# Result products of the first 32 columns over all 128 feature rows, even columns before odd ones, in a dynamic convolution with a maxout block

## The chip, the cores and the metric

The kernel runs on one core of a Trainium2 chip. The metric is the time of one execution on the device in microseconds (us), the median of several runs.

## The reference

Two steps. The first is a dynamic convolution: every position of a sequence has its own 7 weights for each of 8 heads, a softmax of `weight_gen`. The second is a block with two linear maps whose larger value goes on.

```python
# x: (8, 4160, 192), weight_gen: (8, 4160, 8, 7), w1, w2: (192, 1024), w_out: (1024, 192)
w = softmax(weight_gen, axis=-1)                        # with 1e-9 in the denominator
x_pad = zeros(6 rows) followed by x, along the sequence
y[b, s, head] = sum over k in 0..6 of w[b, s, head, k] * x_pad[b, s + k, head]   # 24 features a head
h1 = y @ w1 ; h2 = y @ w2                               # 33280 rows
out = np.maximum(h1, h2) @ w_out                        # float32, (33280, 192)
```

## The kernel before

The 33280 rows lie on the 128 partitions, 260 rows to each. A *column* is one such row on all partitions, so it is 128 rows of the output; there are 260 columns (`NT`). They are worked on in batches of 16 (`BATCHES`), cut into units of 4 columns in the first two batches and of 8 afterwards (`UNITS`).

VectorE (DVE in the profile) multiplies the shifted x by the weights into `m_t` (`mul`, L182) and adds the seven taps into `y_t` (`adds`, L198 to L205). ScalarE (ACT) computes the softmax (L135, L151, L167) and the relus. A DMA transposes `y_t` into `yt` (L214); for the units of 4 columns TensorE (PE) transposes and sums at once instead (`sum_transpose`, L246), and ACT copies the result to `yt` (L253).

The maximum is written as max(h1, h2) = h1 + relu(h2 - h1). So TensorE forms the hidden values `y @ (w2 - w1)` (`hid_tile`, L297), ACT applies the relu (L307, into `rd_t`, with the feature row on the partition), and the result of a column is the sum of two parts in one bank of PSUM: `yt` times the small product w1 @ w_out (`w10`, L349, three products), and `rd_t` times `w_out` (`wo`, L337, in 8 chunks of 128 feature rows).

All products of the main part use half of the array's height: 64 of the 128 rows on which the sum runs. Two of them, one on rows 0 to 63 and one on rows 64 to 127, run side by side, into two different banks. For the results, columns c and c+1 form a pair: `out_first` sums the lower half of the rows into the bank of column c and the upper half into that of column c+1, and `out_second` does the other half of each. Between the two passes a bank goes from one half of the array to the other. `relay` puts an empty ScalarE instruction there, which waits for the last two products of the first pass, and the first two products of the second pass wait for it.

The order of work is written out by hand (a manual schedule). `GROUPS` are two or three hidden tiles each; `hidden` runs one group: all tiles but the last, `out_first` for the columns in turn (`OUTS[g]`, two or four of them), their relus, the relay, the last tile, softmax steps, its relu, `out_second`, and `evac`, the copy of the results from PSUM to `o_t` by ACT (L393), stored by a DMA. The columns 0 to 31 are finished between about 27 and 79 us. At the opening, before 27 us, TensorE runs some products that use the full height: `keep_warm` (L610), `w1_transposed` (L598, its first eight) and `w10_product` (L652).

Of the kernel before, what the change touches and what calls it, by code (L numbers as in the profile page):

```python
# [23 lines left out]
def kernel(  # L24
# [11 lines left out]
    B, S, D = x.shape  # L36
    H, K = weight_gen.shape[2], weight_gen.shape[3]
    F = moe_w1.shape[1]
    P = 128
    PAD = K - 1  # L40
    WGC = H * K
    FCH = F // P
# [190 lines left out]
    def half(j):  # L233
        return slice(64 * j, 64 * j + 64)
# [75 lines left out]
    def column(c):  # L310

        b = min(c // 16, NB - 1)
        for u, (ub, o, n) in enumerate(UNITS):
            if ub == b and o <= c - BATCHES[b][0] < o + n:
                k = c - BATCHES[b][0] - o
                return u, k // 2, k % 2
# [7 lines left out]
    def op_out(c):  # L324

        tile_, at = op_at[c // 2]
        return tile_[:, at + c % 2 * 512:at + c % 2 * 512 + D]

    def out_hidden(c, f, r):

        u, i, j = column(c)
        t0 = TILES.index((u, 0))
        if UNITS[u][2] == 8:
            (rd, k), at = rd_at[t0 + f], j * 512 + i * P
        else:
            (rd, k), at = rd_at[t0 + f // 2], j * 512 + f % 2 * 256 + i * P
        return nc.tensor.matmul(  # L337
            op_out(c), lhsT=rd[half(r), k * 1024 + at:k * 1024 + at + P],
            rhs=wo[half(r), f * D:(f + 1) * D], start=False, stop=(r != j and f == FCH - 1),
            skip_group_check=True,  # L340
        )

    def out_first(now):

        for c in now[::2]:
            u, i, _ = column(c)
            for s in range(3):
                for j in range(2):
                    nc.tensor.matmul(  # L349
                        op_out(c + j),  # L350
                        lhsT=yt_ts[u][half(j), (3 * i + (s + j) % 3) * P:(3 * i + (s + j) % 3 + 1) * P],
                        rhs=w10[half(j), s * D:(s + 1) * D], start=(c == now[0] and s == 0),
                        stop=False, skip_group_check=True,
                    )
            for f in range(FCH):
                last = [out_hidden(c + j, f, j) for j in range(2)]
        return last

    def out_second(now, go):

        for c in now[::2]:
            for f in range(FCH):
                for j in range(2):
                    mm = out_hidden(c + 1 - j, f, j)
                    if c == now[0] and f == 0:
                        tc.add_manual_dep(mm.ins, go.ins.name, SYNC, reason="bank of the other half")

    def relay(last):

        go = nc.scalar.nop()  # L370
        for mm in last:
            tc.add_manual_dep(go.ins, mm.ins.name, SYNC, reason="bank of the other half")
        return go
# [52 lines left out]
    OUTS, c = [[], [], []], 0  # L426
# [8 lines left out]
    def room(g):  # L435

        t0, n = GROUPS[g]
        if "c" in ps:
            for t, k in zip(range(t0, t0 + n), "abc"[:n - 1] + "c"):
                hd_at[t] = ps[k].tile([P, 1024], FP32, name="hd" + k, tag=k), 0  # L440
        else:
            for t in range(t0, t0 + n):
                hd_at[t] = ps["h"].tile([P, 1024], FP32, name="hdp", tag="hd"), 0
        rd = prd.tile([P, 3 * 1024], BF16, name="rd_t", tag="rd")
        for t in range(t0, t0 + n):
            rd_at[t] = (rd, t - t0)
        return rd
# [7 lines left out]
    def hidden(g, now=(), between=lambda: None, beside=lambda: None, ahead=lambda: None,  # L455
               before=lambda: None, after=lambda: None, begun=None):


        t0, n = GROUPS[g]
        rd = begun or room(g)  # L460
        for t in range(t0, t0 + n - 1) if not begun else ():
            hid_tile(t)
        if now:
            out_room(now, "a" if n == 1 and "a" in ps else None)
            last = out_first(now)
        for t in range(t0, t0 + n - 1) if not begun else ():
            relu(rd, t, 1)
        if now:
            go = relay(last)
        hid_tile(t0 + n - 1)  # L470
        before()
        if len(now) > 2:
            beside()
        relu(rd, t0 + n - 1, 1)
        ahead()
        if now:
            out_second(now, go)
            evac(now[0] // 2, len(now) // 2)
        between()
        after()  # L480
        if len(now) <= 2:
            beside()

    def rest_of_results(c):

        parts = [p for p in (c[:4], c[4:-2], c[-2:]) if p]
        assert max(map(len, parts)) <= 4
        go = []
        for i, now in enumerate(parts):
            out_room(now, ("r", "a", "c")[i])  # L490
            go.append(relay(out_first(now)))
            if i:
                out_second(parts[i - 1], go[i - 1])
                evac(parts[i - 1][0] // 2, len(parts[i - 1]) // 2)
        out_second(parts[-1], go[-1])
        evac(parts[-1][0] // 2, len(parts[-1]) // 2)
# [4 lines left out]
    wo = consts.tile([P, FCH * D], BF16, name="wo")  # L501
# [7 lines left out]
    with tc.tile_pool(name="pstage", bufs=1) as pstage:  # L509
# [120 lines left out]
        rd = room(0)  # L630
# [43 lines left out]
        rd = room(3)  # L674
# [11 lines left out]
        sum_transpose(3)  # L686
        out_room(OUTS[3])
        go = relay(out_first(OUTS[3]))
        exp_sum(2)
        red(2)  # L690
        weights(1, 8)
        rd = room(4)
# [113 lines left out]
```

## Time and profile before

| what | value |
|---|---|
| median of 3 runs | 406.31 us (406.18 to 407.36) |
| the profiled execution | 406.16 us, span of its profile 404.3 us |
| TensorE matmul, busy | 397.3 us (98%), 7458 instructions |
| VectorE, busy | 370.3 us (92%) |
| ScalarE, busy | 360.7 us (89%) |
| GpSimd, busy | 76.3 us (19%) |
| L337, the result products | 210.3 us busy, 4160 instructions |
| L297, the hidden products | hda 67.0, hdb 67.0, hdc 67.8 us busy, and hdp at the opening |
| L349, the first part of the results | 55.3 us busy, 780 instructions |

The profile is one execution, taken by the hardware profiler. In its lines PE is TensorE's matmul, PEld its weight load, DVE is VectorE, ACT ScalarE, POOL GpSimd and SP the engine that issues DMAs. A group line gives the source line, the engine, the operation, what is written and read, the shapes (64*128 is the height and width of the array that a matmul uses), how many there are, their busy time and the mean duration of one in ns, and the idle time of the engine before them. Since matmuls are pipelined, their durations overlap; what one costs is the distance from its start to the next start.

### The profile page before, as it was taken

What the parts mean: (1) busy time and instruction counts of PE and PEld (TensorE: products, weight loads), DVE (VectorE), ACT (ScalarE), POOL (GpSimd) and SP (SyncE); (2) the same over time, 40 slices, a digit from 0 to 9 for tenths busy, and PEclk for the clock granted to TensorE, in tenths of its full rate; (3) what the DMA queues carried; (4) which work ended last, traced back from release to release, by engine and by line L of the source; (5) the groups of instructions that cost most, each with busy time, mean ns of one, the idle gap of its engine ahead of it and who ended that gap; (6) DMA issues with size and microseconds to landing.
All of it is one profiled execution on the core that took longest, in us unless ns stands there. A gap on an engine that the chain in (4) does not pass through costs nothing.

```text
span 404.3 us, 16242 instructions
## 1 busy us (share of the span) xinstructions
PE 397.3 (98%) x7458; PEld 318.6 (79%) x7458; DVE 370.3 (92%) x215; ACT 360.7 (89%) x462; POOL 76.3 (19%) x101
## 2 busy tenths in 40 slices
PE   7999999999999999999999999999999999999996
PEld 2699999777777787778777778877787877777795
DVE  5999999999999999999999999999999999999100
ACT  6899999999999989999899999989999899897872
POOL 0311130212222011222221212222012222110000
PEclk9999999999999999999999999999999999999999
DMA  8956549876757855774775587577548647743614
GB/s 250 232 120 184 157 98 245 149 174 155 194 90 232 191 111 121 229 204 78 233 201 109 115 237 203 74 236 200 110 111 240 170 70 241 154 89 51 246 41 158
DMA packets 60785, 65.70 MB, mean 163 GB/s; under 512 B 47631, under 2 KB 49039, under 8 KB 60718
## 3 DMA queue, kind: packets, MB, share of 16 engines
q1 hardware_dynamic: 52334, 40.54, 35.6%
q0 software_dynamic: 8240, 24.04, 29.2%
q8 instruction: 58, 0.95, 0.9%
q10 hardware_dynamic: 144, 0.10, 0.1%
q14 instruction: 9, 0.07, 0.1%
HBM read 35.96 MB, written 25.56 MB: 152 GB/s over the span
## 4 chain that ended last, share of the span: by engine, by line
PE 92%; ACT 3%; DMA 2%; SPq 1%; issue 0%; DVE 0%; DVEq 0%; ACTq 0%
PE op_ps L337 42%; PE hdc L297 13%; PE hda L297 13%; PE hdb L297 13%; PE op_ps L349 8%; PE yps L246 2%; DMA ws1T<-in_moe_w_dram 2%; ACT rd_t L307 1%; PE hdp L297 1%; SPq L544 0%; ACT yt L253 0%; PE pw L652 0%; ACT w1t L670 0%; ACT e_t L135 0%; SPq L536 0%
## 5 line engine op out<-in xcount | busy, mean ns | idle before, releaser
L337 PE MATMUL op_ps<-wo,rd_t 64*128 64x192 bf16 x4160 | 210.3, 243 | 0.0
L337 PEld LDWEIGHTS <-rd_t 64*128 64x128 bf16 x4160 | 180.6, 94 | 15.5
L182 DVE TENSOR_TENSOR m_t<-xb_t,en_t 128x10752 bf16<-128x10752 bf16 (+1 forms) x37 | 187.4, 5070 | 0.3
L297 PEld LDWEIGHTS <-wd 64*128 64x128 bf16 x1776 | 93.4, 94 | 40.1 <-issue 1.1
L307 ACT ACTIVATE rd_t<-hdc 128x1024 bf16<-128x1024 f32 x82 | 84.0, 1024 | 17.6 <-PE hdc L297 15.9
L222 POOL CAST gate<-yt 128x1 f32<-128x1 bf16 x29 | 41.1, 1416 | 267.3 <-DMA yt<-y_t 267.3
L307 ACT ACTIVATE rd_t<-hdb 128x1024 bf16<-128x1024 f32 x81 | 83.6, 1032 | 0.0
L307 ACT ACTIVATE rd_t<-hda 128x1024 bf16<-128x1024 f32 x81 | 83.4, 1030 | 0.0
L198 DVE TENSOR_TENSOR m_t<-m_t 128x4608 bf16<-128x4608 bf16 (+1 forms) x29 | 72.7, 2508 | 0.1
L297 PE MATMUL hdc<-yt,wd 64*128 64x512 bf16 (+1 forms) x534 | 67.8, 359 | 0.0
L393 ACT COPY o_t<-op_ps 128x384 f32<-128x384 f32 (+1 forms) x99 | 56.3, 579 | 12.6 <-PE op_ps L337 12.6
L297 PE MATMUL hda<-yt,wd 64*128 64x512 bf16 (+1 forms) x528 | 67.0, 359 | 0.0
L297 PE MATMUL hdb<-yt,wd 64*128 64x512 bf16 (+1 forms) x522 | 67.0, 362 | 0.0
L349 PE MATMUL op_ps<-w,yt 64*128 64x192 bf16 x780 | 55.3, 243 | 0.0
L349 PEld LDWEIGHTS <-yt 64*128 64x128 bf16 x780 | 38.8, 94 | 15.6 <-issue 0.5
L202 DVE TENSOR_TENSOR m_t<-m_t 128x3072 bf16<-128x3072 bf16 (+1 forms) x29 | 49.9, 1722 | 0.1
L167 ACT ACTIVATE en_t<-wg_t 128x896 bf16<-128x896 f32 (+2 forms) x45 | 35.2, 809 | 2.0 <-PE op_ps L337 2.0
L205 DVE TENSOR_TENSOR y_t<-m_t 128x1536 bf16<-128x1536 bf16 (+1 forms) x29 | 27.3, 941 | 0.5
L114 POOL DMA_DIRECT2D xb_t<-in_x_dram x33 | 18.0, 546 | 21.3 <-DVE m_t L182 10.4
L156 DVE TENSOR_TENSOR wg_t<-wg_t,sum_t 128x280 f32<-128x280 f32 (+5 forms) x46 | 22.0, 481 | 0.0
L147 DVE TENSOR_REDUCE sum_t<-e_t 128x64 f32<-128x448 f32 (+2 forms) x31 | 19.5, 633 | 2.3 <-ACT e_t L135 2.3
L135 ACT ACTIVATE e_t<-wg_t 128x896 f32<-128x896 f32 (+2 forms) x18 | 15.9, 889 | 2.3 <-DMA wg_t<-in_weight_gen_dram 2.3
(49 smaller groups left out, 117.1 us busy)
## 6 DMA issues: line engine op xcount, KB each, us to landing
out_dram<-o_t SPq DMA_DIRECT2D x27, 768.0 KB, 4.5
xb_t<-in_x_dram POOLq DMA_DIRECT2D x30, 384.0 KB, 4.9
wg_t<-in_weight_gen_dram POOLq DMA_DIRECT2D x14, 448.0 KB, 5.6
xb_t<-xb_t POOLq DMA_DIRECT2D x16, 288.0 KB, 5.1
out_dram<-o_t SPq DMA_DIRECT2D x10, 384.0 KB, 3.1
wg_t<-in_weight_gen_dram SPq DMA_DIRECT2D x2, 448.0 KB, 4.2
xs<-in_x_dram SPq DMA_DIRECT2D x2, 384.0 KB, 6.0
xb_t<-in_x_dram POOLq DMA_DIRECT2D x3, 192.0 KB, 4.6
```

The source lines that it names most:

```text
L156: nc.vector.tensor_tensor(out=w_t, in0=w_t, in1=_sub(s_ts[b], hs.start, [[1, hs.stop - hs.start], [0, K]]), op=ALU.subtract)
L167: nc.scalar.activation(out=_sub(en_ts[b], (o * WGC + j * N * K) * 2, [[2 * N, K], [2, N], [1, 2]]), in_=_sub(wg_ts[b], (o * H + j * N) * K ...
L182: return nc.vector.tensor_tensor(out=m_out, in0=x_in, in1=_sub(en_ts[b], o * WGC * 2, [[2, K * n * H], [0, G // 2], [1, 2]]), op=ALU.mult,)
L198: nc.vector.tensor_tensor(out=taps(0, 1, 3), in0=taps(0, 1, 3), in1=taps(3, 1, 3), op=ALU.add)
L202: nc.vector.tensor_tensor(out=taps(0, 2, 2), in0=taps(0, 2, 2), in1=taps(1, 5, 2), op=ALU.add)
L205: nc.vector.tensor_tensor(out=_sub(y_ts[b], o * D, [[64, 2], [P, 3 * w // 2], [1, 64]]), in0=taps(0, 1, 1), in1=taps(2, 1, 1), op=ALU.add,)
L222: nc.gpsimd.tensor_copy(out=gate, in_=yt[:, 0:1])
L297: nc.tensor.matmul(hid_out(t, f, j), lhsT=wd_at(j, s, f // 4, f % 4 * P, P), rhs=_sub(yt_ts[u][half(j), :], (s + j) % 3 * P, [[3 * P, w // ...
L307: relu_of[t0] = nc.scalar.activation(out=rd[:, k * 1024:(k + n) * 1024], in_=hd[:, at:at + n * 1024], func=AF.Relu)
L337: return nc.tensor.matmul(op_out(c), lhsT=rd[half(r), k * 1024 + at:k * 1024 + at + P], rhs=wo[half(r), f * D:(f + 1) * D], start=False, s ...
L349: nc.tensor.matmul(op_out(c + j), lhsT=yt_ts[u][half(j), (3 * i + (s + j) % 3) * P:(3 * i + (s + j) % 3 + 1) * P], rhs=w10[half(j), s * D: ...
L393: nc.scalar.copy(out=_sub(o, c % 24 * D, [[D, len(qs)], [h * D, 2], [1, D]]), in_=_sub(tile_, at + (qs[0] - p) * D, [[D, len(qs)], [512, 2 ...
```

## The change

For columns below 32 (`WHOLE`), `out_hidden` without a half takes all 128 feature rows of a chunk in one product. `out_first` then does the 8 products of the even column c alone, after the same six half-height products of L349 for both columns; `out_second` does the 8 products of the odd column c+1. No bank goes from one half to the other between the passes, and `relay` gives back nothing, so its ScalarE instruction and the two waits on it are gone. From column 32 on all is as it was. Eight more lines in the source move the later line numbers: L337 becomes L338, L349 becomes L352, L393 becomes L401.

```diff
-    def out_hidden(c, f, r):
+    def out_hidden(c, f, r=None):
...
+        rows = slice(0, P) if r is None else half(r)
         return nc.tensor.matmul(
-            op_out(c), lhsT=rd[half(r), k * 1024 + at:k * 1024 + at + P],
-            rhs=wo[half(r), f * D:(f + 1) * D], start=False, stop=(r != j and f == FCH - 1),
+            op_out(c), lhsT=rd[rows, k * 1024 + at:k * 1024 + at + P],
+            rhs=wo[rows, f * D:(f + 1) * D], start=False, stop=(r != j and f == FCH - 1),
             skip_group_check=True,
         )
+
+    WHOLE = 32
...
             for f in range(FCH):
-                last = [out_hidden(c + j, f, j) for j in range(2)]
+                last = [out_hidden(c, f)] if c < WHOLE else [out_hidden(c + j, f, j) for j in range(2)]
         return last
...
         for c in now[::2]:
             for f in range(FCH):
+                if c < WHOLE:
+                    out_hidden(c + 1, f)
+                    continue
                 for j in range(2):
...
     def relay(last):

+        if len(last) == 1:
+            return None
         go = nc.scalar.nop()
```

## The prediction

> **What bounds the kernel now.** I read the shares of busy time first, then the chain that ended last, then who made TensorE wait, then the timeline of TensorE alone.
>
> ```profile
> span 404.3 us, 16242 instructions
> PE 397.3 (98%) x7458; PEld 318.6 (79%) x7458; DVE 370.3 (92%) x215; ACT 360.7 (89%) x462; POOL 76.3 (19%) x101
> PE 92%; ACT 3%; DMA 2%; SPq 1%; issue 0%; DVE 0%; DVEq 0%; ACTq 0%
> L337 PE MATMUL op_ps<-wo,rd_t 64*128 64x192 bf16 x4160 | 210.3, 243 | 0.0
> ```
>
> TensorE (PE) is busy for 98% of the span and is 92% of the chain that ended last. L337, the line that the change edits, is its largest group and has no idle time before it. DVE and ACT are nearly full too, but hardly on the chain. So TensorE time added between 27 us and the end is paid unless a stall of TensorE takes it in. The 243 ns is the life of one matmul in the pipeline and not its price; the price is the distance between starts, which the timeline gives (start, us, then the group):
>
> ```profile
> 19.41 0.62 PE L598 MATMUL tp<-ident,w1E 128*128 128x128 bf16 x8
> 19.96 0.30 PE L598 MATMUL tp<-ident,w1T 64*128 64x64 bf16 x8
> ...
> 24.58 1.48 PE L652 MATMUL pw<-wo,w1t 128*128 128x192 bf16 x16
> 25.99 1.40 PE L246 MATMUL yps<-ident,m_t 64*128 64x64 bf16 x84
> ...
> 27.52 0.84 PE L337 MATMUL op_ps<-wo,rd_t 64*128 64x192 bf16 x16
> 28.18 0.43 PE L349 MATMUL op_ps<-w,yt 64*128 64x192 bf16 x6
> 28.43 0.84 PE L337 MATMUL op_ps<-wo,rd_t 64*128 64x192 bf16 x16
> 29.09 0.83 PE L297 MATMUL hdp<-yt,wd 64*128 64x256 bf16 x12
> 29.74 1.50 PE L337 MATMUL op_ps<-wo,rd_t 64*128 64x192 bf16 x32
> 31.06 0.43 PE L349 MATMUL op_ps<-w,yt 64*128 64x192 bf16 x6
> ```
>
> The reader is to see two things. Eight pairs of half-height matmuls (L337 from 27.52 to 28.18) take 0.66 us, 82.5 ns a pair: the two halves run side by side, the second some 20 ns behind the first. And L652 already does what the change introduces: 128 rows, 192 columns, the same types, wo as the moving side. Its first and last start are 24.581 and 25.815, so a step is 1.234 / 15 = 82.3 ns.
>
> **The products themselves.** Of the first 32 columns (27.5 to 78.8 us) the change takes 32 x 16 = 512 half-height matmuls with their 512 weight loads and puts in 256 full-height ones with 256 loads. That is 256 pairs x 82.5 = 21.12 us against 256 x 82.3 = 21.07: a gain of 0.05 us, nothing. The halves already fill the array.
>
> **Where full height meets half height.** Everything around these products stays at half height: L349, L297, the sums of L246. So each run of full-height products is entered from half height and left to it, which the kernel before never did here. It did so in its opening, seven times. Each time the starts leave a hole that the matmul length does not explain (ends of streaming worked out from the steady step):
> - Leaving: the last full L598 starts at 19.808 and the half-height ones at 19.958: 150 ns where the step is 56, so 94 lost. L652 to L246: 25.815 to 25.993, 178 less 82 is 96. L610 to L246: 311 less 216 is 95.
> - Entering: L246 to L610, 12.848 to 12.971: 123 less 27 is 96. L297 to L598: its last pair starts at 19.185 and 19.205, the next matmul at 19.406; the step of 256 columns is 109, so 201 - 109 = 92 after the later half, and 112 after the first.
> - The other two are longer (314 and 437 ns from start to start), but their first matmul waits for a semaphore, and in the first of them ACT's copies of w1t end at 24.53, just before.
>
> The entering price is 112, not 92: a full-height matmul must wait for the half that trails by 20 ns, and after it the pairs start together, so those 20 ns are not got back. I take 112 in and 96 out.
>
> The Trainium skill, "TensorEngine Tiling (Array Packing)", Key Properties, says that a change of the tiling mode, not merely of the tile, drains the engine; that speaks against this change, and the trace agrees with 92 to 96 ns each time. The skill's "TensorE: Matmul & The Clock Gate", Step-by-step, puts the drain of the array at about 128 cycles, an estimate of 53 ns at its 2.4 GHz; by it the 58 switches below would be 3.1 us, and the sum 408.5. The trace has nothing that short.
>
> **How many switches.** The first 32 columns are 13 groups: three of four columns (0, 16, 22) and ten of two. A group of two has one run of 8 in the first pass and one of 8 in the second, with the last hidden tile between; a group of four has two runs of 8 (L349 stands between them) and one of 16. Runs: 3 x 3 + 10 x 2 = 29, so 58 switches; the built order of TensorE's instructions has the same 29. Four runs are left to L246, whose second pair comes 10 ns late (39 ns after the first at 25.993, not 29). Sum: 29 x (112 + 96) + 4 x 10 = 6.07 us.
>
> **What takes some of it in.** From 27 us on TensorE's matmuls have five holes: 0.28 us (before L246 at 33.57), 0.20 (before L349 at 35.65), 0.20 (inside L246 at 46.86, waiting for nothing that shows), 0.16 (before L349 at 80.28), 0.11 (before L297 at 352.3, put down to the transposed y).
> - 33.57 waits for the result buffer that ACT's copy frees (32.70 to 33.51). ACT runs without a pause there, and the result it copies would come at about 31.7, still in time. Five runs stand before, about 1.0 us, so the hole closes. The next is alike: ACT's copy ends at 35.59, and TensorE would come at about 36.2.
> - 80.28 and 352.3 are transposes at the end of DVE's work. DVE has no idle time between 27 and 377 us, and the pieces of m_t that it overwrites at 40.29 are read by then (L246 ends at 39.09, and 7 runs less two holes put 1.0 us on that: 40.1). So these close too.
> That is 0.28 + 0.20 + 0.16 + 0.11 = 0.75 us given back; the hole at 46.86 I leave as it is.
>
> **The relay.** 13 empty ACT instructions go, each waiting for the end of a first pass. Queued behind them are softmax steps and the relu of the last hidden tile; that relu waits for later TensorE work anyway. ACT's waits on L337 that it removes are 0.9 us in 27 to 90 us, off the chain: I cost it at nothing. The cover is ACT's own lead. If ACT fell behind with TensorE, its weights for DVE would come up to 5.3 us late, and what is late next is the transposed y at 80.28, where TensorE itself arrives 5.3 us later. No DMA and no DVE or POOL instruction changes place.
>
> **Sum.** 6.07 - 0.05 - 0.75 = 5.27 us. The profiled execution took 406.16 us (its span 404.3 and 1.86 around it), 0.15 below the median of 406.31. 406.16 + 5.27 = 411.4; halfway to the median's 411.6 I say 411.5.
>
> **Rivals.**
> - *The switch is dearer here.* For: the longest hole, L610 to L297, loses 437 - 216 = 221 ns. Against: its matmul waits for ACT's copy of yt, which ends at 14.88, 0.05 us before. 58 x 0.221 = 12.8, with 0.8 off: 418.2 us. Chance 0.04.
> - *The hole is half hidden here,* 96 / 2 = 48 ns per switch: 58 x 0.048 = 2.8, less 0.75 is 2.0, about 408.2. For it speaks only that the rows of 192 columns have no entry of their own in the trace. Chance 0.06.
> - *Weight loads stop overlapping.* Full-height loads use the rows that the running matmul uses. If each of the 256 loads, 97 ns in L652, had to wait for its predecessor's end, they would add 24.8 us: 406.2 + 24.8 + 5.3 = 436. Against: L652's loads start 2 ns after the matmul before, and the step stays 82.3. The skill's page on TensorE, Part 3, The mechanism, says that loads overlap running matmuls only where the row group differs; L652 contradicts it. Chance 0.02.
> - *Not slower.* The opening's holes could belong to its new operands (each of the seven switches is also a change of tile and source) and not to the height. Then nothing is added, and a relay that no longer holds ACT could close the holes at 33.57 and 35.65, which are ACT's: 406.16 - 0.05 - 0.48 = 405.6 us. It decides if the hole at a switch is under 0.5 / 58 = 9 ns. Against: in the same stage changes of source without a change of height cost nothing (L337 to L349 to L337 to L297 at 28.18, 28.43, 29.09 keep the step to within 4 ns). Chance 0.04.
>
> **Numbers.** The forecast has the other 0.84. Its own bounds: 58 x 94 ns less all five holes (0.95) is 4.5, or 410.7; 6.07 with no hole closed is 412.2; the runs before spread over 1.2 us upward. The low end goes halfway from 410.7 to the half-hidden hole's 408.2, 409.5; the high end adds half of that spread to 412.2, 412.8. Left out are the rivals, 0.16 together. No change means within 0.3%, 1.2 us, which is about what a measurement of this kernel can tell. Slower: 0.84 + 0.06 + 0.04 + 0.02 = 0.96; the last rival is 0.03 same and 0.01 faster.
>
> **What would show it.** Right: in the page after, L338 twice (64 rows x3648, 128 rows x256); TensorE starts 200 ns after the first half of the last pair when it enters a full run and 178 ns after the last full matmul when it leaves; the stretch from 27.3 to the 32nd column's end (78.8 us) longer by about 5.5 us; after it the same step as before, and no hole at 80 us. Wrong: entries and exits under 30 ns; a step of full matmuls other than 82 ns; or new holes of TensorE with ACT or DVE as releaser after 80 us.

## The result, and the profile after

The changed kernel took 412.22 us (median of 6 runs, 411.31 to 416.24), the kernel before 406.99 us (6 runs, 406.18 to 409.23): 5.23 us more, a ratio of 1.0116 with a 95% interval of 1.0076 to 1.0156, which is 3.1 to 6.3 us. The profiled execution took 412.46 us, with a span of 410.7. The forecast was 411.5 us in 409.5 to 412.8, 5.27 us more.

The page of the changed kernel: busy shares, the chain that ended last by engine, and, from the groups of TensorE with shapes kept apart, the two forms of the edited line.

```profile
span 410.7 us, 15717 instructions
PE 402.7 (98%) x7202; PEld 303.1 (74%) x7202; DVE 370.9 (90%) x215; ACT 362.0 (88%) x462; POOL 72.7 (18%) x101
PE 93%; DMA 2%; DVE 2%; SPq 1%; issue 1%; ACT 0%; DVEq 0%
```

```profile
L338 PE MATMUL op_ps<-wo,rd_t 64*128 64x192 bf16 x3648 | 181.2, 243 | 0.0
L338 PE MATMUL op_ps<-wo,rd_t 128*128 128x192 bf16 x256 | 26.2, 247 | 0.0
```

TensorE is still the chain, still busy for 98%, and has 256 matmuls fewer in a longer span. Matmul busy time does not show the loss as idle time, since a matmul's recorded life in the pipeline (243 to 247 ns) is longer than the distance to the next start and covers the holes. The timeline does (start, us, then the group), and so does the list of waits between 27 and 90 us (total, times, longest) for the weight loads:

```profile
36.73 0.82 PE L297 MATMUL hdp<-yt,wd 64*128 64x256 bf16 x12
37.39 0.41 PE L352 MATMUL op_ps<-w,yt 64*128 64x192 bf16 x6
37.73 0.83 PE L338 MATMUL op_ps<-wo,rd_t 128*128 128x192 bf16 x8
38.50 0.83 PE L297 MATMUL hdp<-yt,wd 64*128 64x256 bf16 x12
39.26 0.83 PE L338 MATMUL op_ps<-wo,rd_t 128*128 128x192 bf16 x8
40.02 1.40 PE L246 MATMUL yps<-ident,m_t 64*128 64x64 bf16 x84
41.26 0.82 PE L297 MATMUL hdp<-yt,wd 64*128 64x256 bf16 x12
```

```profile
PEld L338 <- issue: 5.9, 29, 0.4
PEld L297 <- issue: 3.3, 21, 0.2
PEld L246 <- issue: 0.8, 5, 0.2
PEld L352 <- issue: 0.6, 4, 0.2
```

From start to start, L352 takes 0.34 us here and took 0.25 as L349 before, L338 takes 0.77 and took 0.66, L297 between two full-height runs 0.76 and took 0.66. Each gains about 0.1 us at its end, wherever the height changes next; L297 with no change behind it (36.73, 41.26) keeps 0.66. The weight loads of L338 start late 29 times: once for each run of full-height products. The other 30 are the 29 ends of these runs and the opening's last change of height, at 27.13. The waits name no other engine ("issue").

The opening is not touched by the change, and yet it moves: the first L246 after the full-height L652 (L660 in the changed file) starts at 25.99 us in the profile before and at 27.13 after. In the profiles of the experiments below, but for the last, it lies between 26.3 and 28.9, and the medians of the kernel before move from 406.99 to 408.13 us with the session. So the comparisons below are made in the traces, from that L246 to the last start of a matmul: 374.20 us before and 379.44 after, 5.24 us more.

The two ways of comparing do not agree everywhere. For the change itself the medians give 5.23 us. For the experiments the distance between the medians is 0.5 to 1.7 us smaller than that in the traces, and for four of them (one run a group, all columns, the first 16, the middle) the distance in the traces lies above the 95% interval of the measured ratio. The medians contain the opening, which moves by up to 3 us from one profile to the next; the traces are one execution each. What part of the opening's movement goes into which median is not shown.

### The profile page after: what moved, and what is told of

Its sections match the earlier page's. It is cut to its first block, busy times and chain, and to the rows that moved or that the text cites. A ratio compares the mean times of both kernels' runs of the same rounds, so it can differ in the third digit from the quotient of the medians.

```text
span 410.7 us, 15717 instructions
## 1 busy us (share of the span) xinstructions
PE 402.7 (98%) x7202; PEld 303.1 (74%) x7202; DVE 370.9 (90%) x215; ACT 362.0 (88%) x462; POOL 72.7 (18%) x101
## 4 chain that ended last, share of the span: by engine, by line
PE 93%; DMA 2%; DVE 2%; SPq 1%; issue 1%; ACT 0%; DVEq 0%
PE op_ps L338 43%; PE hdc L297 13%; PE hda L297 13%; PE hdb L297 13%; PE op_ps L352 8%; PE yps L246 2%; DMA ws1T<-in_moe_w_dram 2%; PE hdp L297 2%; DVE m_t L182 1%; SPq L552 0%; PE pw L660 0%; DVE sum_t L147 0%; SPq L544 0%; SPq L526 0%; DVE wd L587 0%
## 5 line engine op out<-in xcount | busy, mean ns | idle before, releaser
L338 PE MATMUL op_ps<-wo,rd_t 64*128 64x192 bf16 (+1 forms) x3904 | 207.4, 243 | 0.0
L338 PEld LDWEIGHTS <-rd_t 64*128 64x128 bf16 (+1 forms) x3904 | 174.0, 94 | 23.0 <-issue 5.9
L297 PEld LDWEIGHTS <-wd 64*128 64x128 bf16 x1776 | 82.3, 94 | 50.0 <-issue 4.0
L222 POOL CAST gate<-yt 128x1 f32<-128x1 bf16 x29 | 37.3, 1286 | 272.9 <-DMA yt<-y_t 272.9
L401 ACT COPY o_t<-op_ps 128x384 f32<-128x384 f32 (+1 forms) x99 | 55.9, 575 | 13.5 <-PE op_ps L338 13.5
L297 PE MATMUL hdc<-yt,wd 64*128 64x512 bf16 (+1 forms) x534 | 66.6, 359 | 0.0
L297 PE MATMUL hda<-yt,wd 64*128 64x512 bf16 (+1 forms) x528 | 65.8, 359 | 0.0
L297 PE MATMUL hdb<-yt,wd 64*128 64x512 bf16 (+1 forms) x522 | 65.7, 361 | 0.0
L352 PE MATMUL op_ps<-w,yt 64*128 64x192 bf16 x780 | 53.5, 243 | 0.0
L352 PEld LDWEIGHTS <-yt 64*128 64x128 bf16 x780 | 35.5, 94 | 18.2 <-issue 0.6
```

What stands on the lines that cost most here:

```text
L222: nc.gpsimd.tensor_copy(out=gate, in_=yt[:, 0:1])
L297: nc.tensor.matmul(hid_out(t, f, j), lhsT=wd_at(j, s, f // 4, f % 4 * P, P), rhs=_sub(yt_ts[u][half(j), :], (s + j) % 3 * P, [[3 * P, w // ...
L338: return nc.tensor.matmul(op_out(c), lhsT=rd[rows, k * 1024 + at:k * 1024 + at + P], rhs=wo[rows, f * D:(f + 1) * D], start=False, stop=(r ...
L352: nc.tensor.matmul(op_out(c + j), lhsT=yt_ts[u][half(j), (3 * i + (s + j) % 3) * P:(3 * i + (s + j) % 3 + 1) * P], rhs=w10[half(j), s * D: ...
L401: nc.scalar.copy(out=_sub(o, c % 24 * D, [[D, len(qs)], [h * D, 2], [1, D]]), in_=_sub(tile_, at + (qs[0] - p) * D, [[D, len(qs)], [512, 2 ...
```

## The experiments

The theory: every change of the array's height costs TensorE a fixed hole of about 0.1 us, so about 0.21 us for each run of full-height products, and up to 0.95 us of older holes, as the prediction counted them, is given back. The rivals: the full-height product itself is dear; the missing relay, or the order of even and odd columns, is; only the early columns, where ACT has no pause, are touched. "Above before" in the readings is the distance in the traces just described; the measured medians stand beside it, each with the kernel before in the same session.

### One chunk of eight at full height

```diff
             for f in range(FCH):
-                last = [out_hidden(c, f)] if c < WHOLE else [out_hidden(c + j, f, j) for j in range(2)]
+                if c < WHOLE and f == 0:
+                    out_hidden(c, f)
+                    continue
+                last = [out_hidden(c + j, f, j) for j in range(2)]
...
+        for c in now[::2]:
+            if c < WHOLE:
+                out_hidden(c + 1, 0)
         for c in now[::2]:
-            for f in range(FCH):
-                if c < WHOLE:
-                    out_hidden(c + 1, f)
-                    continue
+            start = 1 if c < WHOLE else 0
+            for f in range(start, FCH):
```

> Of the eight chunks of a column only the first is one full-height product; the other seven are half-height pairs as before, and the relay stays. The full-height products fall from 256 to 32, the runs of them stay 29. If a change of height is what costs (about 0.21 us for a run, in and out), the time stays at the changed kernel's, 5.2 us above before, between 4.5 and 6.0. If a full-height product is what costs, 32 of 256 of it are left: 0.7 us above before. If the missing relay or the order of even and odd columns is what costs, about nothing is left: within 0.5 us of before.

Measured: 5.24 us above before; 412.31 us against 407.60 (ratio 1.0097, 1.0062 to 1.0132). Its groups of TensorE by shape:

```profile
L338 PE MATMUL op_ps<-wo,rd_t 64*128 64x192 bf16 x4096 | 204.7, 243 | 0.0
L338 PE MATMUL op_ps<-wo,rd_t 128*128 128x192 bf16 x32 | 7.7, 255 | 0.0
```

An eighth of the full-height products, with the relay back in, loses the same to 0.01 us. The price goes with the runs, of which there are 29 in both, and not with the products, the relay or the order. Here full height and half height also follow each other within L338, on the same operands, and yet from the one full-height product to the next start it is 188 ns (28.188 to 28.376) where a step is 82, so the holes do not need a change of operand or source line.

### Runs of the first pass cut in two

```diff
             for s in range(3):
+                if s == 1 and c < WHOLE:
+                    for f in range(4):
+                        out_hidden(c, f)
                 for j in range(2):
...
-            for f in range(FCH):
+            for f in range(4 if c < WHOLE else 0, FCH):
```

> The changed kernel with each run of eight in the first pass cut in two: four products after the first pair of the three small products, four after the other two pairs. The same 256 full-height products in 45 runs instead of 29. If a change of height costs: 16 x 0.21 = 3.4 us more than the changed kernel, 8.6 above before (7.8 to 9.4). If a full-height product costs, or the relay, or the order: the same as the changed kernel, 5.2 above before.

Measured: 8.64 us above before; 415.64 us against 407.60 (1.0183, 1.0138 to 1.0227). Sixteen more runs of the same products cost 3.40 us more, 0.212 us each.

```profile
28.88 0.26 PE L355 MATMUL op_ps<-w,yt 64*128 64x192 bf16 x2
29.07 0.51 PE L338 MATMUL op_ps<-wo,rd_t 128*128 128x192 bf16 x4
29.51 0.34 PE L355 MATMUL op_ps<-w,yt 64*128 64x192 bf16 x4
29.78 0.50 PE L338 MATMUL op_ps<-wo,rd_t 128*128 128x192 bf16 x4
```

In this timeline four products take 0.44 us to the next start (29.07 to 29.51); at 82.5 ns they would take 0.33.

### One run a group

```diff
+            if c < WHOLE:
+                continue
             for f in range(FCH):
-                last = [out_hidden(c, f)] if c < WHOLE else [out_hidden(c + j, f, j) for j in range(2)]
+                last = [out_hidden(c + j, f, j) for j in range(2)]
+        for c in now if now[0] < WHOLE else ():
+            for f in range(FCH):
+                last = [out_hidden(c, f)]
...
         hid_tile(t0 + n - 1)
+        early_out = now and now[0] < WHOLE
+        if early_out:
+            evac(now[0] // 2, len(now) // 2)
```

The second pass is empty for these columns, and `evac` is not repeated after it.

> The changed kernel with all full-height products of a group in one run, in the first pass (even and odd columns of it), and the copy of the results ahead of the last relu: 256 products in 13 runs. If a change of height costs: 13 x 0.21 = 2.8 us less the 0.95 us of holes that were given back, 1.8 us above before (1.0 to 3.0; the moved copy may add or save some tenths). If a full-height product costs: 5.2 above before, as the changed kernel.

Measured: 2.30 us above before; 409.31 us against 407.60 (1.0023, 0.9994 to 1.0052). The same 256 products in 13 runs cost less than half. It is half a microsecond over the 1.8 expected, and holes account for it: the one that was 0.11 us at 352.3 before is 0.33 here at 356.46, where the hidden products wait for the transposed y, and there are two new ones of 0.06 and 0.05 us at 49.79 and 92.78. That the moved copy of the results makes them is possible and not shown.

```profile
356.45 0.98 PEld L297 LDWEIGHTS <-wd 64*128 64x128 bf16 x12 [0.38 <-DMA yt<-y_t]
```

### The relay left in

```diff
-        if len(last) == 1:
-            return None
         go = nc.scalar.nop()
...
-                    out_hidden(c + 1, f)
+                    mm = out_hidden(c + 1, f)
+                    if c == now[0] and f == 0:
+                        tc.add_manual_dep(mm.ins, go.ins.name, SYNC, reason="as before")
                     continue
```

> The changed kernel with the relay left in: an empty ScalarE instruction waits for the last product of the even columns, and the first product of the odd columns waits for it. If the relay is free, as the prediction has it: the same as the changed kernel within 0.3 us, 5.2 above before. If the relay's absence saves something that the changes of height hide, or holds the second pass: 0.3 to 1.5 us more than the changed kernel, at worst 13 x 0.1 us.

Measured: 5.23 us above before; 412.20 us against 407.60 (1.0099, 1.0061 to 1.0137). The relay is worth nothing in either direction.

### All columns, the first 16, and 36 in the middle

Three small edits: `WHOLE = NT`; `WHOLE = 16`; and in place of `c < WHOLE` the test `96 <= c < 132`.

> The change for all 260 columns: 217 runs of full-height products instead of 29, no relay anywhere. If a change of height costs: 217 x 0.21 = 46.3 us less 0.95 of holes, 45 us above before (43 to 48), since DVE and ACT then have slack everywhere. If the loss came from the early columns alone (ACT without a pause there, the opening): 5 to 6 us above before.

> The change for the first 16 columns: 15 runs. 15 x 0.213 = 3.2 us less the holes. All holes fall behind these columns or in them, so if TensorE being late closes them: 3.2 - 0.95 = 2.25 us above before (1.6 to 2.9). If holes are not closed: 3.2. If the loss is in proportion to the columns with no holes: 2.6.

> The change for the 36 columns 96 to 131 instead of the first 32: 30 runs in a stretch in which TensorE has no hole, with only the hole at 352 us (0.11) behind it. If the holes of the early stretch are what takes 0.8 us of the loss there: 30 x 0.213 - 0.11 = 6.3 us above before, 1.0 more than the changed kernel (5.9 to 6.8). If the holes play no part: 30 / 29 of the changed kernel's loss, 5.4.

Measured: all columns 45.08 us above before (452.12 us against 408.13, ratio 1.1057, 1.1024 to 1.1091); the first 16 columns 2.49 (409.35 us, 1.0024, 1.0003 to 1.0045); the middle 6.62 (413.05 us, 1.0111, 1.0079 to 1.0142).

```profile
L338 PE MATMUL op_ps<-wo,rd_t 128*128 128x192 bf16 x2080 | 209.4, 247 | 0.0
L182 DVE TENSOR_TENSOR m_t<-xb_t,en_t 128x10752 bf16<-128x10752 bf16 (+1 forms) x37 | 187.4, 5071 | 12.2 <-ACT en_t L167 11.9
```

The loss goes on at the same rate far from the early columns; there (groups of the kernel with all columns) DVE waits 11.9 us for ACT's weights and it costs nothing, since TensorE is later still. What the two smaller edits cost turns on the older holes. The table gives the price of one run, once the holes of over 0.04 us that a trace still has are counted (the kernel before has 0.93 us, without one of 0.05 that nearly all have at the first L349). A hole is the distance from the first start of the last pair before it to the next start, less the usual step.

| kernel | runs | above before, us | holes left, us | (above + 0.93 - left) / runs |
|---|---|---|---|---|
| the change | 29 | 5.24 | 0 | 0.213 |
| one chunk of eight | 29 | 5.24 | 0 | 0.213 |
| first pass cut in two | 45 | 8.64 | 0 | 0.213 |
| one run a group | 13 | 2.30 | 0.44 | 0.215 |
| all columns | 217 | 45.08 | 0 | 0.212 |
| first 16 columns | 15 | 2.49 | 0.25 | 0.211 |
| columns 96 to 131 | 30 | 6.62 | 1.06 | 0.216 |

One price fits 13 to 217 runs. The middle came out 0.3 us over the expected 6.3: its hole in L246, 0.17 us before, was 0.51 there. It stands inside a group of 84 matmuls:

```profile
46.43 0.77 PE L246 MATMUL yps<-ident,m_t 64*128 64x64 bf16 x41
47.55 0.81 PE L246 MATMUL yps<-ident,m_t 64*128 64x64 bf16 x43 [0.35 <-issue]
```

The waits name no engine for it, but its place says something. 2241 recorded instructions of TensorE stand before it, here and in the kernel before. A hole of 0.10 us in L246 in the kernel with the first 16 columns (at 29.96) stands after 961, and one of 0.45 us in the last experiment below (at 85.90) after 3009. These places differ by multiples of 256. The pages list a queue of instruction transfers, 16 KB each (packets, MB, share), here of the kernel before, with 14,923 recorded instructions of TensorE, and of the kernel with all columns, with 10,763:

```profile
q8 instruction: 58, 0.95, 0.9%
q8 instruction: 42, 0.69, 0.6%
```

That is one transfer for each 256 instructions, and in each of the four traces one had landed 1.25 to 1.48 us before the hole ended. So the hole looks like a wait for the next block of TensorE's own instructions, in the line whose matmuls follow each other fastest (29 ns a pair). No run tests this by itself. The kernel with the first 16 columns has such a place in its opening too: after 705 instructions TensorE's weight loads stand still for 1.06 us, until 25.71, and this opening is the longest of those above.

### What the hole follows

The kernel before with extra products on the identity in its opening, shape by shape:

```diff
         keep_warm(30)
+        for M in (128, 64, 32):
+            for _ in range(6):
+                for _ in range(4):
+                    nc.tensor.matmul(warm[0:M, 0:256], lhsT=ident[:, 0:M], ...)
+                for _ in range(4):
+                    for j in range(2):
+                        nc.tensor.matmul(warm[0:M, j * 512:j * 512 + 256], lhsT=ident[half(j), 0:M], ...)
...
```

> The kernel before with extra products on the identity in its opening, of no use to the result: four full-height and four half-height products in turn, 256 columns each, six times over, with a stationary side of 128, then 64, then 32 columns; then the same with the lower half alone in place of pairs. Its total time says nothing; the starts do. The hole at a change of height is about as long as a weight load of 128 columns (95 ns). If it is a weight load that can't be done ahead across a change of height, it shrinks with the stationary side: about 48 ns at 64 columns and 24 at 32. If the array runs empty before it changes height, it stays at 90 to 100 ns at all three. If entering costs 20 ns more because of the trailing half, the entries from the lower half alone lose 92 to 96 ns against the last start, and pairs 112 against their first half.

Its one execution took 444.7 us. The timeline of stretches at 128, 64 and 32 stationary columns, and weight loads at 64 and at 32:

```profile
11.50 0.61 PE L617 MATMUL warm<-ident 128*128 128x256 bf16 x4
12.04 0.61 PE L621 MATMUL warm<-ident 64*128 64x256 bf16 x8
12.59 0.61 PE L617 MATMUL warm<-ident 128*128 128x256 bf16 x4
...
19.15 0.62 PE L617 MATMUL warm<-ident 128*64 128x256 bf16 x4
19.70 0.62 PE L621 MATMUL warm<-ident 64*64 64x256 bf16 x8
...
23.58 0.61 PE L617 MATMUL warm<-ident 128*32 128x256 bf16 x4
24.12 0.61 PE L621 MATMUL warm<-ident 64*32 64x256 bf16 x8
```

```profile
19.15 0.36 PEld L617 LDWEIGHTS <-ident 128*64 128x64 bf16 x4 [0.20 <-issue]
23.58 0.33 PEld L617 LDWEIGHTS <-ident 128*32 128x32 bf16 x4 [0.20 <-issue]
```

Four steps of 109 ns would be 0.44 us; a stretch takes 0.54, and 0.55 at 64 columns. The last start before a change and the first after it lie 205 ns apart on leaving full height and 202 on entering it at 128 columns, 203 and 199 at 64 and at 32: 90 to 96 ns more than a step, at every width. That was to tell an array that must run empty from a weight load that can't be done ahead.

The recorded loads do not shrink with the width as the expectation had assumed, but at 64 columns they are longer, and that tells where a load shows:

| stationary columns | a load, median, ns (half height, full height) | hole, ns (entering, leaving) | first step after a change, ns (later steps: 109) |
|---|---|---|---|
| 128 | 94, 98 | 93, 96 | 120 |
| 64 | 107, 110 | 90, 94 | 133 to 134 |
| 32 | 93, 97 | 90, 94 | 119 to 120 |

Where the loads are 12 to 13 ns longer, the first step after the change is 13 to 14 ns longer, and the hole before it is not. So the hole is not the length of a load; the load shows in the 10 to 24 ns by which the first step is long. The same 10 ns stand behind the hole at 46.86 in the kernel before, where no height changes (39 ns where a step is 29). In the records the first load of the new height starts at the end of the hole, 2 to 5 ns before its matmul (in the changed kernel at 37.727 and 37.731), while within a run each load starts some 2 ns after the matmul before. So the loads are not done ahead across a change, but what they wait for lies before them. An array that must run empty fits this; no view shows the array itself, so this stays a reading. The hole keeps to 90 to 97 ns at all the sizes tried: 64, 128, 192, 256 or 512 columns streamed, 32 to 128 columns stationary, one half or two.

The part on the trailing half did not come as expected. Entries from a lower half alone lose 90 to 93 ns, but pairs lose only 93 to 96 against their first half and not 112: the pairs stand 3 to 4 ns apart here, so there was nothing trailing.

## Why the prediction was right, point by point

- *The products are free.* A run of 16 lasts 0.66 us longer than one of 8 (1.426 against 0.766), 82.5 ns a product, the same as a pair. The gain of 0.05 us was not there, and nothing hung on it.
- *The switches.* 58 of them, and their sum with the holes counted, 5.24 + 0.93 = 6.17 us, against 6.07 worked out. The opening's five clean rows gave the price for the whole kernel.
- *The split of that price was wrong, though its sum was right.* The prediction had 112 ns in, 20 of them for the trailing half, and 96 out. After a change of height the pairs run 3 to 4 ns apart (L352 at 37.552 and 37.556), so entering L338 at 37.731 loses 96 ns against the first half, as leaving does (38.318 to 38.497, 179 less 82). In place of the 20 there are about 10 ns at each change: the first step after it is long (37.731 to 37.823, 92 ns, where the next are 82 and 83). The prediction had put these 10 ns on the four exits to L246 alone. In all 96 + 10 + 96 + 10 = 212 ns a run, against 208. Only the first entry (L352 to L338 at 28.78), with a pair 19 ns apart before it, lost the 112 of the prediction.
- *The holes.* Four were to close and the one at 46.86 was left as it was; in the changed kernel all five are gone, 0.93 us, where 0.75 was predicted for four. The fifth is 0.17 us; the 0.20 of the prediction is the distance between two starts with the step still in it.
- *Luck.* The closeness of the sum is in part luck: 6.17 - 0.93 = 5.24 us against 6.07 - 0.05 - 0.75 = 5.27. The switches cost 0.10 more than worked out and no gain of 0.05 shows, and the fifth hole gave 0.17 back that was not counted on.
- *The relay* costs nothing: 5.23 with it, 5.24 without.
- *Cover.* DVE did come to wait, for ACT's weights, logarithms and exponentials (1.0, 1.2 and some 0.5 us); TensorE was late by more and met no hole.
- *What would show it.* Leaving came at 178 to 179 ns, entering at 178 to 179 from L352's first half and 205 from that of an L297 of 256 columns, 200 having been named. From the first L349 to the first start behind column 31 the stretch grew from 51.54 to 57.05 us, the 5.5 that was named, and the rest of the run shrank by 0.27, the holes at 80.28 and 352.3.
- *The rivals.* A hole of half the size falls with the table, and so does the dearer switch of 221 ns; dearer weight loads fall with the first experiment, the not slower case with both.

## What to carry to other kernels

Two half-height products side by side and one full-height product took the same time here (82.5 ns at 192 columns), so joining them buys fewer instructions and no time on TensorE. Mixing heights costs: here 0.21 us for each stretch of the other height, the same for 1 product in it or 32, so count the stretches and not the products, and if both heights are needed, put all of one together. A price seen a handful of times in a kernel's opening, always the same, is good enough to multiply, provided that the rows that also wait for something are set apart.

## What the runs showed that was not expected

- After a change of height the two halves run 3 to 4 ns apart instead of 17 to 20, and the first step is 10 ns long (92 instead of 82). With 64 stationary columns it is 24 ns long, as the loads are longer there.
- The records of weight loads do not get shorter with fewer stationary columns: 93 to 97 ns at 32, 107 to 110 at 64, 94 to 98 at 128; and the hole does not follow them.
- A hole of 0.10 to 0.51 us inside L246 (46.86 before, 47.55 in the kernel with columns 96 to 131) comes and goes with what runs before it. In four traces its places lie multiples of 256 instructions of TensorE apart, as many as come with one instruction transfer; that TensorE waits for its instructions there is likely and not tested.
